# Moving the 64-row products of an MLP's first half next to the 64-row products of a recurrent cell

## The chip, the cores and the metric

The kernel runs on one core of a Trainium2 chip. Its engines work in parallel, each in its own order of instructions, and meet at semaphores: TensorE (PE in the profile) does matrix products, VectorE (DVE) and ScalarE (ACT) work element by element, GpSimd (POOL) does the same[...], and SyncE (SP) issues the transfers (DMAs). Products read their operands from SBUF and write to PSUM[...]. The metric is the device time of one execution in microseconds; the time of a kernel is the median of its runs.

## The reference

Two blocks follow each other, both in float32. The first is an mLSTM cell for 4 batches, 8 heads, 768 steps and a head size of 40. In essence:

```python
for t in range(S):
    m_new = np.maximum(f_gate[:, :, t] + m, i_gate[:, :, t])
    f_stab = np.exp(f_gate[:, :, t] + m - m_new)
    i_stab = np.exp(i_gate[:, :, t] - m_new)
    C = f_stab * C + i_stab * outer(v[t], k[t])
    n = f_stab * n + i_stab * k[t]
    y[t] = sigmoid(o[t]) * (C @ q[t]) / max(abs(n @ q[t]), 1)
```

The heads are then put side by side into x, 768 rows of 320 for each batch. The second block mixes and applies an MLP:

```python
u = x + real(fft(fft(x, axis=1), axis=2))
un = (u - mean(u)) / sqrt(var(u) + 1e-06)      # over the last axis
out = u + maximum(un @ w_ch1, 0) @ w_ch2       # 320 -> 1280 -> 320
```

## The kernel before, in words

**The recurrent cell** is computed in chunks: 768 steps are six chunks of 128 (c = 0 to 5). Within a chunk the steps act on each other through a 64-row matrix of scores, and the past comes in through a state. For batches 2 to 4 a chunk is treated as two halves of 64 steps, so that all its products are small ones of 64 or 40 rows on a quarter of PE's array (`product`, L519). A *recurrent group* is what PE does for one chunk in one slot: `halves_from_state` (L683), `halves_from_chunk` in two turns (L694), with a tiny read by ACT between them (`halves_between`, L699) and, with them, the next chunk's `halves_scores` (L635) and `halves_to_state` (L643). Around it, DVE adds to the state (`halves_add`, L667), weighs the scores (`halves_weigh`, L672) and makes the output (`mlstm_finish`, L712 to L720); POOL lets the state decay (`halves_decay`, L652), scales the queries (qg, L501) and the values (vw, L507) and masks (L515); ACT makes exponentials. The rows of the output that lie one step off are moved by SyncE and POOL in `halves_rows` (L731, L732).

**The mix** folds x into even and odd parts on DVE (`mix_fold`, L815 to L822; for later batches also `mix_fold_again`), transforms along both axes with products on PE, adds on DVE (`mix_add`, L952 to L966) and turns the centred result over, into the feature-major arrays `uT`.

**The MLP's first half** multiplies 320 features by 320x1280 weights. 320 is 128 + 64 + 128 rows: two *full* products of 128 rows and one *rest* of 64 rows. Two rests share PE's array, each in its own half of the rows (`w1t_sb` holds them). The 1280 hidden features form ten blocks of 128, taken in pairs n = 0 to 4; the 768 rows form two groups (gr = 0, 1) of 384. For batch 1, `mlp_in` (L1059) issues the full products of a pair, and its inner function `between` (L1050) the pair's rests behind them, or at the start of the next pair. For batches 2 to 4, `mlp_block` does a pair in four steps in the manner of Strassen: seven full products (L1121) in place of eight, with sums of the weights and of the inputs; the sums of inputs come from DVE (`mlp_sums`, L1109: T3 in buffer e, uT in place, T2 in buffer raw, T4 in buffer m). Step 2 ends with four rests (`tails`, L1126) and with three additions on DVE (`add`, L1130). Four PSUM banks, pm0 to pm3, hold the results; the first product of pair i + 1 (`begin`) takes the bank of pair i that `add(h12, p3)` has read last.

**Order.** Everything is in one order that is written by hand: `at(slot, phase, function, ...)` puts a call into a plan and `run` issues the calls sorted by slot and phase, the phases being EVAC 0, FILL 1, MAIN 2 and FILL_PE 3 with fractions between. Each engine executes its instructions in that order. A slot is roughly one step of an MLP. Batch 1's MLP begins at slot 31, the next ones 32 slots later each. The recurrent cell of batch b + 1 and its mix run in the slots of batch b's MLP: the cells begin at slots 32, 53 and 83, a chunk every three slots (`plan_halves`). `x_done` are the slots from which the mix may fold. The PSUM banks that the first MLP takes are written out as a string of digits (`turn`, in `bank`).

Of the kernel before, what the change touches and what calls it, by code (L numbers as in the profile page):

```python
# [19 lines left out]
L = 128  # L20
# [33 lines left out]
def kernel(  # L54
# [69 lines left out]
    def at(slot, phase, fn, *args):  # L124
        plan.setdefault((slot, phase), []).append((fn, args))
# [633 lines left out]
            at(t, FILL_PE + (2.5 if c < 4 else 1), mlstm_turn, b, c, c < 4)  # L759
            at(x, FILL + 0.05, mlstm_finish, b, c)  # L760

    def plan_halves(b, s0, stride=3):
        for c in range(NT):
            s = s0 + stride * c
            t = 22 + 2 * c if b == 1 and c < 3 else s - 5
            at(t, FILL, mlstm_load, b, c)
            at(t, FILL, mlstm_load_max, b, c)
            at(34 if b == 1 and c == 2 else t + 1, FILL, mlstm_load_decay, b, c)
            at(s - 1, FILL, mlstm_load_o, b, c)
            at(s - 1, FILL, mlstm_scale_v, b, c)  # L770
            at(s - 1, FILL + 0.3, mlstm_exp, b, c, 0)
            at(s, FILL, mlstm_exp, b, c, NP)
            at(s, FILL_PE + 2.05, halves_scores, b, c)
            at(s, FILL_PE + 2.5, halves_to_state, b, c)
            for i in range(2):
                at(s + i, FILL + 0.05, halves_decay, b, c, i)
                at(s + 1 + i, FILL - 0.2, halves_add, b, c, i)
            at(s, FILL + 0.1, mlstm_scale_q, b, c)
            at(s + 1, FILL, mlstm_mask, b, c)
            if (b, c) == (3, 2):  # L780
                at(s + 2, MAIN + 0.1, halves_weigh, b, c)
            else:
                at(s + 1, FILL + 0.55 if b == 1 and c > 0 else MAIN + 0.7, halves_weigh, b, c)
            end = c == NT - 1
            at(s + 3, MAIN - 0.1 if end else FILL_PE, halves_from_state, b, c)
            at(s + 3, MAIN - 0.1 if end else FILL_PE, halves_from_chunk, b, c, 0)
            at(s + 3, MAIN if end else FILL_PE + 0.5, halves_between, b, c)
            at(s + 3, FILL_PE + 3, halves_from_chunk, b, c, 1)
            at(s + 3, FILL_PE + 0.6, mlstm_tanh, b, c)
            at(s + (5 if (b, c) == (2, 2) else 4), {(2, 4): FILL + 0.3, (3, 3): FILL - 0.3}.get((b, c), FILL + 0.3 if b == 1 else MAIN + 0.55), mlstm_finish, b, c)  # L790
            at(s + 6, FILL - 0.6, halves_rows, b, c)

    class Mix:
        def __init__(self):
            self.pu, self.uc, self.pt, self.po = {}, {}, {}, {}

    mixes = {}  # L800

# [208 lines left out]
    def plan_mix(b, s0, x_done, s_feat, s_add, s_turn):  # L1010
        for j in range(TG):
            p = TG - 1 - j
            at(x_done[j] + (b > 1 and j == TG - 1), FILL + 0.5 if b < 2 else FILL_PE + 0.2, mix_fold, b, p)
            if b == 0:
                at((s0 - 4, s0 - 2, s0)[j], FILL_PE + 4, mix_seq, b, p, (0, 1))
                at((s0 - 2, s0 - 2, s0)[j], FILL_PE + 4, mix_tail, b, p)
            elif b == 1 or j == 0:
                if b > 1:
                    for step, slot in enumerate((x_done[0], x_done[-1] + 2, x_done[-1] + 6)):
                        at(slot, FILL_PE + 0.25, mix_fold_again, b, step)  # L1020
                at(s0, FILL_PE + 4, mix_seq, b, p, (0,))
                at(s0 + 1, FILL_PE + 4, mix_seq, b, p, (1,))
                at(s0 + 2, FILL_PE + 4, mix_tail, b, p)
        for i in range(2):
            at(s0 + 1 if b == 0 else s0 + 1 + i, FILL, mix_seq_out, b, i)
        at(s0 + (1 if b == 0 else 3), FILL + 0.1, mix_tail_out, b)
        for p in range(TG):
            at(s_feat[p], FILL_PE + 4, mix_feat, b, p)
        for c, a, t in zip(ORDER, s_add, s_turn):
            at(a, FILL if b < 2 else MAIN - 0.3 if c == 0 else MAIN + 0.5, mix_add, b, c)  # L1030
            at(t, FILL + 0.1, mix_center, b, c)
            at(t, FILL_PE + (5 if b == 0 or c in ORDER[:4] else -0.1), mix_turn, b, c)
            if b > 0:
                at(t, FILL_PE + 6, mix_turn_out, b, c)
            elif t < s_mlp:
                at(t + 1, FILL + 0.2, mix_turn_out, b, c)
            else:
                at(t + 1, EVAC, mix_turn_out, b, c)


    def mlp_in(b, gr, f):


        k = mixes[b]
        u = [uT_bufs[gr][:, ch].rearrange("p c t -> p (c t)") for ch in range(3)]

        def between(pm, n, start):
            for i in range(2):
                r = slice(i * TAIL, (i + 1) * TAIL)
                nc.tensor.matmul(pm[i], w1t_sb[r, n * L:(n + 1) * L], u[1][r], start=start, stop=not start,  # L1050
                                 skip_group_check=True)


        ahead = gr == 1 and f // 2 in (1, 3)
        if f % 2 == 0:
            k.pm = k.pm_next if ahead else [bank("pm", [L, TG * L]) for _ in range(2)]
        for i, ch in ((1, 1),) if f % 2 else ((0, 0), (0, 1), (1, 0)):
            f0 = (f // 2 * 2 + i) * L
            nc.tensor.matmul(k.pm[i], w1_sb[:, ch, f0:f0 + L], u[2 * ch], start=(ch == 0 and not ahead),  # L1059
                             stop=(ch == 1 and ahead), skip_group_check=True)  # L1060
        if f % 2 and not ahead:
            between(k.pm, f // 2, False)
            if gr == 1 and f // 2 < NFF // 2 - 1:
                k.pm_next = [bank("pm", [L, TG * L]) for _ in range(2)]
                between(k.pm_next, f // 2 + 1, True)


    hid = {}
# [1 line left out]
    def hidden(gr, f):  # L1070
        return hid[gr, f % 2][:, f // 2 * TG * L:(f // 2 + 1) * TG * L]

    def mlp_relu(b, gr, f):
        nc.scalar.activation(out=hidden(gr, f), in_=mixes[b].pm[f % 2], func=AF.Relu, scale=-1.0)

# [35 lines left out]
    def mlp_block(b, i, step):  # L1111
# [30 lines left out]
        if step == 0:  # L1142
            if i == 0:
                begin(0)
            k.pm = [k.p1, bank("pm", [L, TG * L], banks[1])]
            product(k.pm[1], A[0, 1], mlp_u(0, 2), True)
        elif step == 1:
            k.pm.append(bank("pm", [L, TG * L], banks[2]))
            p1, _, p5 = k.pm
            if i == 0:  # L1150
                product(p5, A[1, 0], mlp_u(1, 0), True)
            product(p1, block(w1x["S2"], i), T2)
            nc.scalar.copy(out=h12, in_=p1)
            if i > 0:
                product(p5, A[1, 0], mlp_u(1, 0), True)
            add(h12, p5)
        elif step == 2:
            k.pm.append(bank("pm", [L, TG * L], banks[3]))
            p1, p2, p5, p3 = k.pm
            product(p3, block(w1x["S4"], i), mlp_u(1, 2), True)  # L1160
            product(p1, block(w1x["S3"], i), T3)
            nc.scalar.copy(out=h22, in_=p1)
            tails(1, (p3, p5))
            tails(0, (p2, p1))
            add(h12, p3)
# [326 lines left out]
```

## Time and profile before

Three runs took 391.72 us in the median (391.14 to 392.08). The profiled execution took 392.19 us, 390.4 of them in the span that the profile covers.

| | before |
|---|---|
| median of the runs | 391.72 us |
| profiled execution | 392.19 us |
| span of the profile | 390.4 us |
| PE busy | 379.6 us, 4174 products |
| DVE busy | 278.0 us |
| ACT busy | 172.1 us |
| POOL busy | 134.9 us |
| granted clock of PE | full in all slices |

The first halves of the MLPs of batches 1, 2 and 3 lie, together with recurrent groups, at about 59 to 112, 163 to 204 and 249 to 286 us of the span. In these stretches PE is busy for 52.37 of 53.00, 40.36 of 41.00 and 36.16 of 37.00 us. Batch 4's MLP follows to the end, at 390.4 us.

In a line of the timeline, the first number is the start in microseconds from the beginning of the span, the second the length, then come engine, line of the kernel, operation and operands; `128*128` is the part of PE's array that a product uses (rows by columns), and `[0.35 <-DVE uT L1109]` an idle time ahead of the line and what ended it. A float32 product appears as two records. The ends of products are modelled, so starts are more exact than ends.

### The profile page before, as it was taken

The numbers are of one execution on the slowest core, as the hardware profiler recorded it, in microseconds if no ns is written. First come the engines' busy times: TensorE is split into PE (matmuls) and PEld (weight loads), VectorE is DVE, ScalarE is ACT, GpSimd is POOL, SyncE is SP. The second block draws the span as 40 slices with busy tenths as digits, with TensorE's granted clock in tenths as the row PEclk, the third lists the DMA queues.
The fourth block names the chain that finished last, engine by engine and source line by source line (L and its number), as shares of the span: only waits on it lengthen the run. The fifth ranks groups of instructions, "written<-read, shape, count | busy, mean of one in ns | idle before, by whom it ended". The sixth has DMA issues, their size and how long they took to land.

```text
span 390.4 us, 10585 instructions
## 1 busy us (share of the span) xinstructions
PE 379.6 (97%) x4174; PEld 277.3 (71%) x4174; DVE 278.0 (71%) x671; ACT 172.1 (44%) x481; POOL 134.9 (35%) x237
## 2 busy tenths in 40 slices
PE   8999899999999999999999999999999999999996
PEld 6777555656667777765569998755588996556996
DVE  7789988499599587476975699777655785346652
ACT  6887357477543233655462314554530133545000
POOL 5739504467954442173254134541500000020000
PEclk9999999999999999999999999999999999999999
DMA  7887499579394345437700626400000000000101
GB/s 224 287 235 204 159 254 255 179 214 271 109 231 116 122 116 150 149 102 184 182 2 28 174 80 192 135 20 2 0 2 34 6 30 34 2 0 0 35 34 35
DMA packets 25631, 44.78 MB, mean 115 GB/s; under 512 B 5727, under 2 KB 14766, under 8 KB 25454
## 3 DMA queue, kind: packets, MB, share of 16 engines
q1 hardware_dynamic: 25582, 44.11, 38.9%
q8 instruction: 33, 0.54, 0.6%
q14 instruction: 16, 0.13, 0.1%
HBM read 38.49 MB, written 4.12 MB: 109 GB/s over the span
## 4 chain that ended last, share of the span: by engine, by line
PE 78%; DVE 14%; issue 3%; ACT 3%; POOL 1%; DVEq 0%; ACTq 0%; POOLq 0%
PE po L1240 20%; PE pm L1121 15%; PE po L1184 8%; PE pm L1059 7%; PE ph L519 4%; PE pm L1126 4%; PE pu L938 4%; PE ps L519 3%; PE pm L1050 2%; PE put L981 2%; PE pz L907 1%; PE pz L895 1%; DVE h L1130 1%; DVE so L716 1%; PE pM L221 1%
## 5 line engine op out<-in xcount | busy, mean ns | idle before, releaser
L1190 DVE SCALAR_TENSOR_TENSOR x<-po,rstd,x 128x160 f32<-128x160 f32 (+1 forms) x69 | 27.1, 394 | 37.4 <-PE po L1240 32.5
L1130 DVE TENSOR_TENSOR h<-h,pm 128x384 f32<-128x384 f32 x60 | 30.5, 548 | 27.1 <-PE pm L1121 12.6
L652 POOL TENSOR_TENSOR C<-C,decB 128x164 f32<-128x164 f32 x30 | 15.9, 531 | 67.5 <-DVE C L667 56.1
L1121 PE MATMUL pm<-uT,w_sb 128*128 128x384 f32 x90 | 37.7, 506 | 1.3 <-DVE uT L1109 0.6
L491 ACT ACTIVATE W<-W,colT 128x64 f32<-128x64 f32 x144 | 37.5, 339 | 0.4 <-DMA W<-M_d 0.4
L1184 PE MATMUL po<-w_sb,h 128*128 128x320 f32 x120 | 34.3, 435 | 0.0
L515 POOL TENSOR_SCALAR_AFFINE_SELECT W<-W 64x512 f32<-64x512 f32 x36 | 27.3, 759 | 10.6 <-ACT W L491 9.1
L1005 POOL TENSOR_TENSOR t<-rstd 128x6 f32<-128x6 f32 x12 | 3.3, 273 | 79.9 <-DVE v L999 79.4
L1059 PE MATMUL pm<-uT,w_sb 128*128 128x384 f32 x80 | 29.2, 500 | 0.1
L1184 PEld LDWEIGHTS po<-w_sb,h 128*128 128x128 f32 x120 | 22.3, 190 | 9.5 <-issue 0.6
L1240 PE MATMUL po<-T,S 128*128 128x160 f32 x180 | 27.8, 301 | 0.3 <-DVE x L1190 0.3
L501 POOL TENSOR_TENSOR qg<-qk,Gb 128x512 f32<-128x512 f32 (+1 forms) x21 | 27.1, 1290 | 1.7 <-DMA qk<-in_qkT 1.6
L1240 PEld LDWEIGHTS po<-T,S 128*128 128x128 f32 x180 | 25.5, 190 | 1.7 <-DVE x L1190 0.5
L1121 PEld LDWEIGHTS pm<-uT,w_sb 128*128 128x128 f32 x90 | 15.5, 189 | 15.6 <-DVE h L1130 6.7
L1240 PE MATMUL po<-w_sb,h 128*128 128x160 f32 x180 | 26.3, 300 | 0.0
L1240 PEld LDWEIGHTS po<-w_sb,h 128*128 128x128 f32 x180 | 25.2, 190 | 1.4 <-DVE x L1190 0.3
L986 ACT COPY uT<-put 128x384 f32<-128x384 f32 x24 | 11.2, 477 | 30.1 <-PE put L981 30.1
L507 POOL TENSOR_TENSOR vw<-kvt,colT 128x328 f32<-128x328 f32 x23 | 19.7, 859 | 13.1 <-DMA qk<-in_qkT 10.1
L1177 ACT ACTIVATE h<-h 128x384 f32<-128x384 f32 x45 | 23.1, 520 | 2.0 <-DVE h L1130 2.0
L1126 PE MATMUL pm<-uT,w1t_sb 64*128 64x384 f32 x120 | 23.4, 508 | 0.0
L1059 PEld LDWEIGHTS pm<-uT,w_sb 128*128 128x128 f32 x80 | 14.1, 189 | 9.6 <-issue 1.9
L974 ACT ACTIVATE uc<-x 128x384 f32<-128x384 f32 x24 | 14.4, 613 | 12.6 <-DVE x L966 11.1
(241 smaller groups left out, 843.4 us busy)
## 6 DMA issues: line engine op xcount, KB each, us to landing
kvt<-in_kv SPq DMA_DIRECT2D x24, 336.0 KB
qk<-in_qkT SPq DMA_DIRECT2D x48, 160.0 KB
raw<-in_w SPq DMA_DIRECT2D x10, 640.0 KB
Gb<-G_d SPq DMA_DIRECT2D x36, 128.0 KB
W<-M_d SPq DMA_DIRECT2D x36, 128.0 KB
so<-in_o SPq DMA_DIRECT2D x24, 160.0 KB
out<-x SPq DMA_DIRECT2D x24, 160.0 KB
x<-so SPq DMA_DIRECT2D x9, 140.0 KB
```

The costliest lines, as they stand in the source:

```text
L491: nc.scalar.activation(out=k.W[:, h, :], in_=M, func=AF.Exp, scale=-1.0, bias=colT[:, c, 0, b * H + h:b * H + h + 1])
L501: nc.gpsimd.tensor_tensor(out=k.qg[:, :, t], in0=k.qk[:, 0, :, t], in1=k.Gb[:, :, t], op=OP.mult)
L515: nc.gpsimd.affine_select(out=W, in_=W, compare_op=OP.is_ge, fill=0.0, base=base, pattern=[[0, H], [step, LH]], channel_multiplier=-1)
L519: nc.tensor.matmul(out, w, x, start=start, stop=True, skip_group_check=True)
L1059: nc.tensor.matmul(k.pm[i], w1_sb[:, ch, f0:f0 + L], u[2 * ch], start=(ch == 0 and not ahead), stop=(ch == 1 and ahead), skip_group_check= ...
L1121: nc.tensor.matmul(bank, w, u, start=start, stop=True, skip_group_check=True)
L1126: nc.tensor.matmul(bank, block(w1t_sb, i)[rows], mlp_u(gr, 1)[rows], start=False, stop=True, skip_group_check=True)
L1130: nc.vector.tensor_tensor(out=h, in0=h, in1=bank, op=OP.add)
L1177: nc.scalar.activation(out=h, in_=h, func=AF.Relu, scale=-1.0)
L1184: nc.tensor.matmul(k.po[gr, i], hidden(gr, f)[:, i * L:(i + 1) * L], w2_sb[:, f, :], start=(f == 0), stop=(f == NFF - 1))
L1190: nc.vector.scalar_tensor_tensor(out=u, in0=po, scalar=k.rstd[:, c:c + 1], in1=u, op0=OP.mult, op1=OP.add)
L1240: nc.tensor.matmul(po, a[:, f], w[:, f], start=start and f == 0, stop=f == half - 1, skip_group_check=True)
```

## The change

Rests move to recurrent groups, or recurrent groups to rests. No product is added or removed, and each is computed on the same operands.

1. *Batch 1.* `between` goes. A new function `mlp_tails` issues the two rests of a pair, and a table of slots puts it ahead of or behind recurrent groups. `TAILS_AHEAD` lists the pairs whose rests open the sum in the bank, `TAILS_BEHIND` those whose rests close it; for the others they come in the middle. The banks are kept by pair (`k.pm`), and the last relus of the first group of rows stand one slot later.
2. *Batches 2 to 4, MLP.* In `mlp_block`, the rests and the three additions become a step of their own (3) in the same slot, at phase MAIN + 0.05; what was step 3 becomes step 4. Slots are counted as before.
3. *Cells of batches 3 and 4.* `plan_halves` takes the starts of the chunks from a table in place of a stride of three. Batch 3's last two groups come one and two slots later, batch 4's last three 2, 3 and 4 slots later. A chunk's output groups stand at the next chunk's start (`o`), and the last one at MAIN + 0.02, just ahead of the rests.
4. `x_done` of batch 4 and the last step of `mix_fold_again` are fitted to that.

```diff
-    def plan_halves(b, s0, stride=3):
+    def plan_halves(b, s0):
+        starts = [s0 + n for n in ((0, 3, 6, 9, 12, 15, 18), (0, 3, 6, 9, 12, 16, 20), (0, 3, 6, 9, 14, 18, 22))[b - 1]]
         for c in range(NT):
-            s = s0 + stride * c
+            s, o = starts[c:c + 2]
...
-            at(s + 3, MAIN - 0.1 if end else FILL_PE, halves_from_state, b, c)
-            at(s + 3, MAIN - 0.1 if end else FILL_PE, halves_from_chunk, b, c, 0)
-            at(s + 3, MAIN if end else FILL_PE + 0.5, halves_between, b, c)
-            at(s + 3, FILL_PE + 3, halves_from_chunk, b, c, 1)
-            at(s + 3, FILL_PE + 0.6, mlstm_tanh, b, c)
-            at(s + (5 if (b, c) == (2, 2) else 4), {(2, 4): FILL + 0.3, (3, 3): FILL - 0.3}.get((b, c), FILL + 0.3 if b == 1 else MAIN + 0.55), mlstm_finish, b, c)
-            at(s + 6, FILL - 0.6, halves_rows, b, c)
+            at(o, MAIN + 0.02 if end else FILL_PE, halves_from_state, b, c)
+            at(o, MAIN + 0.02 if end else FILL_PE, halves_from_chunk, b, c, 0)
+            at(o, MAIN + 0.03 if end else FILL_PE + 0.5, halves_between, b, c)
+            at(o, FILL_PE + 3, halves_from_chunk, b, c, 1)
+            at(o, FILL_PE + 0.6, mlstm_tanh, b, c)
+            at(o + (2 if (b, c) == (2, 2) else 1), {(2, 4): FILL + 0.3, (3, 3): FILL - 0.3}.get((b, c), FILL + 0.3 if b == 1 else MAIN + 0.55), mlstm_finish, b, c)
+            at(o + 3, FILL - 0.6, halves_rows, b, c)
...
-                    for step, slot in enumerate((x_done[0], x_done[-1] + 2, x_done[-1] + 6)):
+                    for step, slot in enumerate((x_done[0], x_done[-1] + 2, x_done[-1] + (6 if b == 2 else 5))):
...
-        def between(pm, n, start):
...
-        ahead = gr == 1 and f // 2 in (1, 3)
-        if f % 2 == 0:
-            k.pm = k.pm_next if ahead else [bank("pm", [L, TG * L]) for _ in range(2)]
+        if f % 2 == 0 and (gr, f // 2) not in k.pm:
+            k.pm[gr, f // 2] = [bank("pm", [L, TG * L]) for _ in range(2)]
+        pm, ahead, tailed = k.pm[gr, f // 2], (gr, f // 2) in TAILS_AHEAD, (gr, f // 2) in TAILS_BEHIND
...
-        if f % 2 and not ahead:
-            between(k.pm, f // 2, False)
-            if gr == 1 and f // 2 < NFF // 2 - 1:
-                k.pm_next = [bank("pm", [L, TG * L]) for _ in range(2)]
-                between(k.pm_next, f // 2 + 1, True)
...
+    TAILS_AHEAD, TAILS_BEHIND = ((0, 1), (1, 2)), ((0, 0), (0, 3), (0, 4), (1, 1), (1, 4))
+
+    def mlp_tails(b, gr, n):
+
+        k = mixes[b]
+        ahead, last = (gr, n) in TAILS_AHEAD, (gr, n) in TAILS_BEHIND
+        if ahead:
+            k.pm[gr, n] = [bank("pm", [L, TG * L]) for _ in range(2)]
+        for i in range(2):
+            r = slice(i * TAIL, (i + 1) * TAIL)
+            nc.tensor.matmul(k.pm[gr, n][i], w1t_sb[r, n * L:(n + 1) * L], uT_bufs[gr][r, 1].rearrange("p c t -> p (c t)"),
+                             start=ahead, stop=last, skip_group_check=True)
...
             nc.scalar.copy(out=h22, in_=p1)
+        elif step == 3:
+            p1, p2, p5, p3 = k.pm
             tails(1, (p3, p5))
             tails(0, (p2, p1))
             add(h12, p3)
...
-            for step in range(4):
-                at(s, MAIN, mlp_block, b, i, step)
-                s += 1
+            for step in range(5):
+                at(s, MAIN + 0.05 * (step == 3), mlp_block, b, i, step)
+                s += step != 2
...
-                    at(s, EVAC, mlp_relu, b, gr, f - 1)
-                    at(s, EVAC, mlp_relu, b, gr, f)
+                    late = gr == 0 and f == NFF - 1
+                    at(s + late, EVAC, mlp_relu, b, gr, f - 1)
+                    at(s + late, EVAC, mlp_relu, b, gr, f)
+        if b == 0:
+            for slot, phase, gr, n in ((1, 0.05, 0, 0), (1, 4.5, 0, 1), (4, 0.05, 0, 2), (7, 0.05, 0, 3), (10, 0.05, 0, 4),
+                                       (10, 0.05, 1, 0), (13, 0.05, 1, 1), (13, 0.05, 1, 2), (16, 0.05, 1, 3), (19, 0.05, 1, 4)):
+                at(s_mlp + slot, MAIN + phase, mlp_tails, b, gr, n)
...
-        done = [s_mlstm + n for n in ((16, 19, 22) if b == 0 else (18, 21, 22))]
+        done = [s_mlstm + n for n in ((16, 19, 22) if b == 0 else (20, 23, 24) if b == 3 else (18, 21, 22))]
```

More of the change, by code (lines that the diff above doesn't have):

```diff
@@ L784, in plan_halves @@
             end = c == NT - 1
-            at(s + 3, MAIN - 0.1 if end else FILL_PE, halves_from_state, b, c)
-            at(s + 3, MAIN - 0.1 if end else FILL_PE, halves_from_chunk, b, c, 0)
-            at(s + 3, MAIN if end else FILL_PE + 0.5, halves_between, b, c)
-            at(s + 3, FILL_PE + 3, halves_from_chunk, b, c, 1)
-            at(s + 3, FILL_PE + 0.6, mlstm_tanh, b, c)
-            at(s + (5 if (b, c) == (2, 2) else 4), {(2, 4): FILL + 0.3, (3, 3): FILL - 0.3}.get((b, c), FILL + 0.3 if b == 1 else MAIN + 0.55), mlstm_finish, b, c)
-            at(s + 6, FILL - 0.6, halves_rows, b, c)
+            at(o, MAIN + 0.02 if end else FILL_PE, halves_from_state, b, c)
[5 more added lines that the diff above has]
+            at(o + 3, FILL - 0.6, halves_rows, b, c)
     class Mix:
         def __init__(self):
-            self.pu, self.uc, self.pt, self.po = {}, {}, {}, {}
+            self.pu, self.uc, self.pt, self.po, self.pm = {}, {}, {}, {}, {}
     mixes = {}
@@ L1045, in mlp_in @@
         u = [uT_bufs[gr][:, ch].rearrange("p c t -> p (c t)") for ch in range(3)]
-        def between(pm, n, start):
[L1048 to L1051, printed above, removed]
-        ahead = gr == 1 and f // 2 in (1, 3)
-        if f % 2 == 0:
-            k.pm = k.pm_next if ahead else [bank("pm", [L, TG * L]) for _ in range(2)]
+        if f % 2 == 0 and (gr, f // 2) not in k.pm:
+            k.pm[gr, f // 2] = [bank("pm", [L, TG * L]) for _ in range(2)]
+        pm, ahead, tailed = k.pm[gr, f // 2], (gr, f // 2) in TAILS_AHEAD, (gr, f // 2) in TAILS_BEHIND
         for i, ch in ((1, 1),) if f % 2 else ((0, 0), (0, 1), (1, 0)):
             f0 = (f // 2 * 2 + i) * L
-            nc.tensor.matmul(k.pm[i], w1_sb[:, ch, f0:f0 + L], u[2 * ch], start=(ch == 0 and not ahead),
-                             stop=(ch == 1 and ahead), skip_group_check=True)
-        if f % 2 and not ahead:
-            between(k.pm, f // 2, False)
-            if gr == 1 and f // 2 < NFF // 2 - 1:
-                k.pm_next = [bank("pm", [L, TG * L]) for _ in range(2)]
-                between(k.pm_next, f // 2 + 1, True)
+            nc.tensor.matmul(pm[i], w1_sb[:, ch, f0:f0 + L], u[2 * ch], start=(ch == 0 and not ahead),
+                             stop=(ch == 1 and not tailed), skip_group_check=True)
+    TAILS_AHEAD, TAILS_BEHIND = ((0, 1), (1, 2)), ((0, 0), (0, 3), (0, 4), (1, 1), (1, 4))
[8 more added lines that the diff above has]
+                             start=ahead, stop=last, skip_group_check=True)
     hid = {}
@@ L1073, in mlp_relu @@
     def mlp_relu(b, gr, f):
-        nc.scalar.activation(out=hidden(gr, f), in_=mixes[b].pm[f % 2], func=AF.Relu, scale=-1.0)
+        nc.scalar.activation(out=hidden(gr, f), in_=mixes[b].pm[gr, f // 2][f % 2], func=AF.Relu, scale=-1.0)
     def block(t, n):
```

## The prediction

> **What bounds the kernel now.** First the page's head, its busy shares and its chain by engine, to see whether one engine sets the end.
>
> ```profile
> span 390.4 us, 10585 instructions
> PE 379.6 (97%) x4174; PEld 277.3 (71%) x4174; DVE 278.0 (71%) x671; ACT 172.1 (44%) x481; POOL 134.9 (35%) x237
> PE 78%; DVE 14%; issue 3%; ACT 3%; POOL 1%; DVEq 0%; ACTq 0%; POOLq 0%
> ```
>
> TensorE (PE) is busy for 97% of the span and carries most of the chain. So a nanosecond saved in PE's stream shortens the run, if nothing PE waits for becomes late. "Busy" includes the gaps in which PE changes the shape of its products, so they must be read from starts of instructions. The timeline of PE in batch 1's MLP, taken line by line (start, length, engine, group):
>
> ```profile
> 75.50 0.92 PE L1050 MATMUL pm<-uT,w1t_sb 64*128 64x384 f32 x4
> 76.35 0.55 PE L981 MATMUL put<-ident,uc 128*128 128x128 f32 x3
> 76.73 2.75 PE L1059 MATMUL pm<-uT,w_sb 128*128 128x384 f32 x8
> 79.41 0.92 PE L1050 MATMUL pm<-uT,w1t_sb 64*128 64x384 f32 x4
> 80.25 0.68 PE L519 MATMUL ph<-C,qg 40*64 40x41 f32 x32
> ```
>
> Rests (64*128, called T below) stand between full products (F, 128*128), recurrent groups (R, 64*64 and 40*64) elsewhere. One fp32 product is two records. From one record's start to the next: full to full 322.5 ns, but last full to first rest 416 (+93); first pair of rests to the next 420 instead of 316 (+104): entering T costs 197 ns. Leaving T costs 97 + 104 = 201. T to R costs 97 + 22 = 119, F to R 93 + 22 = 115, R to F 118 + 104 = 222. R to T occurs nowhere: bounds 115 (the cheapest switch seen) and 319 (R's exit and both parts of T's entry, 118 + 201); I take 222, as R to F.
>
> Next the waits that come near PE: VectorE (DVE) in the first-half stages. PE, then DVE, then POOL at the start of batch 3's MLP:
>
> ```profile
> 248.40 1.45 PE L1121 MATMUL pm<-uT,w_sb 128*128 128x384 f32 x4
> 249.78 0.68 PE L519 MATMUL ph<-C,qg 40*64 40x41 f32 x32
> 250.27 0.42 PE L519 MATMUL ph<-kvt,W 64*64 64x41 f32 x16
> 250.50 0.67 PE L519 MATMUL ps<-qk 40*64 40x64 f32 x32
> 251.00 0.51 PE L519 MATMUL ps<-vw,kvt 64*40 64x41 f32 x32
> 251.32 0.42 PE L519 MATMUL ph<-kvt,W 64*64 64x41 f32 x16
> 252.08 0.91 PE L1121 MATMUL pm<-uT,w_sb 128*128 128x384 f32 x2 [0.35 <-DVE uT L1109]
> ```
>
> ```profile
> 249.65 0.81 DVE L1109 TENSOR_TENSOR e<-uT 128x384 f32<-128x384 f32 x1
> 250.50 1.53 DVE L1109 TENSOR_TENSOR uT<-uT,uT 128x384 f32<-128x384 f32 x1
> 252.06 0.88 DVE L1109 TENSOR_TENSOR raw<-uT 128x384 f32<-128x384 f32 x1
> ```
>
> ```profile
> 249.59 0.46 POOL L652 TENSOR_TENSOR C<-C,decB 128x164 f32<-128x164 f32 x1
> 250.02 1.59 POOL L501 TENSOR_TENSOR qg<-qk,Gb 128x512 f32<-128x512 f32 x1
> 251.57 1.90 POOL L515 TENSOR_SCALAR_AFFINE_SELECT W<-W 64x512 f32<-64x512 f32 x2
> ```
>
> A recurrent group fills the time in which DVE forms the sums that PE needs. Those sums take 0.81, 1.53 and 0.88 us; alone (batch 2, from 163.87) each takes 0.56. Their ends follow POOL's: the two engines alternate.
>
> **What the Trainium skill says.** "TensorEngine Tiling (Array Packing)", Key Properties: changing the tiling mode drains TensorE, changing the tile within a mode does not. The trace agrees: 93 to 118 ns at every change of shape, and 7 ns between the two row halves of a pair of rests. "TensorE: Matmul & The Clock Gate", Part 3, The mechanism: weights are loaded ahead only where the row groups do not conflict; here the load of 79.408 starts 2 ns before its product, after a switch. "SBUF — State Buffer", Who interferes with whom: a DVE instruction with two SBUF inputs contends with a GpSimd one that reads SBUF, and the first to start holds the port for its whole length; the 1.53 us beside qg's 1.59 agree.
>
> **The change part by part.** No product is added or removed; the rests are moved until they touch recurrent groups. Counting neighbours in the order of PE's instructions, before and after: F to T 23 to 19, R to F 23 to 19, F to R 19 to 11, T to F 18 to 10, T to R 5 to 13, R to T 0 to 4. The sum is −4×0.197 − 4×0.222 − 8×0.115 − 8×0.201 + 8×0.119 + 4×0.222 = −2.36 us: 12 switches fewer, 0.197 each, six in batch 1's MLP, three each in batch 2's and 3's. With R to T at 115 ns it is −2.79, at 319 it is −1.97.
>
> Batch 1's MLP (59 to 112 us): −1.18. The first product of group (0,3) used to follow a pair of rests; now it directly follows the recurrent group. Its bank is read by DVE's L958 of the mix, which ends at 76.06 where R ended at 74.50. Before, PE came to it 2.23 us after R; now 2.23 minus the rests and their switches (about 0.94) = 1.29, while DVE frees the bank at 1.56 plus a handover of 0.07: a wait of +0.34. Behind it on PE stands the rest of the stage. Other covers thin without vanishing: the weighing (L672) of chunk 4 ends at 103.68 for a use at 104.83 and PE comes 0.98 earlier; the last piece of the second weights (L426) ends 0.6 to 0.75 ahead of need. ACT's warm-up wait of 0.50 at 82.48 stays. Net −0.84 (bounds −1.18 if the bank is free in time, −0.4 if the last cover goes too).
>
> Batch 2's MLP (163 to 204): −0.59 of switches. Gone with the order: two lags of 0.063 into the next block (179.69, 187.56) and a warm-up wait of about 0.4 (176.75): −0.52. New: batch 3's last finish (L712 to L720) stands, in block 3, ahead of the folding. DVE's queue from the last rest of block 2 to the release of block 3's first bank:
>
> ```profile
> 192.75 1.56 PE L1126 MATMUL pm<-uT,w1t_sb 64*128 64x384 f32 x8
> 194.53 0.91 PE L1121 MATMUL pm<-uT,w_sb 128*128 128x384 f32 x2 [0.21 <-DVE h L1130]
> ```
>
> DVE needs 1.27 (adds) + 1.59 (finish) + 1.59 (fold) + 0.90 (L1212) + 0.55 (L994 to L999) + 0.46 (add) + 1.59 (fold) + 0.60 (add and handover) = 8.56 us; PE is there after R8 0.78 + fourteen full records 4.30 + rests 1.50 + switches 0.41 = 6.99. PE waits 1.57 instead of 0.29: +1.28. Net +0.17.
>
> Batch 3's MLP (249 to 286): the group at 249.78 now stands two slots later. PE is free at 249.69 and the sums stand bare. POOL's order becomes the two one-row copies (L731, L732), vw of chunk 4 (L507), decay, qg. The copies end at 249.6, DVE's L1190 at 249.74: I take vw as first. It holds the port for about 0.65 of its median 0.74 us (records overlap by some 0.1), to 250.25; then in turn e 0.5 (to 250.75), decay 0.35, uT 0.5 (to 251.6), qg 1.0 (my estimate of its part not spent waiting, from the median of 1.27), raw 0.55 (to 253.15); the product with raw starts at 253.2: stalls of 2.87 us against 0.59 before, +2.28. Without the group's DVE and POOL work three waits fall (257.20, 262.69, 273.28: 0.38 + 0.16 + 0.15 = −0.69). Block 3 has the same late finish without L1212: 7.65 − 6.99 = 0.66 against 0.06, +0.60. Switches −0.59. Net +1.60. If DVE starts first, raw is ready at 252.1 and the net is +0.5.
>
> Batch 4's MLP is unchanged. DMA issues move with the groups, on SyncE: the loads of batch 3's last chunk and of batch 4's chunks 4 and 5 by one to three slots, as far as their readers do; the row moves of batch 4's chunk 3 by two slots, three slots ahead of the fold that reads them. DMA engines are busy for 8% of 249 to 286 us and hide them. Without that cover a landing would delay that fold; the page gives no landing time, so the bounds are nothing and one slot, about 1.5 us. I take nothing.
>
> Sum: −0.84 + 0.17 + 1.60 = +0.93 us on the profiled 392.19 (span 390.4 and 1.8 outside it). The median shown, 391.72, lies 0.47 below, so the forecast is 391.72 + 0.93, about 392.6.
>
> **The rivals.** Measurement can tell 0.2%, 0.78 us, from no change.
> 1. The switches are saved and the waits are covered: PE's lead in these stages is made by DVE work that moves away together with the group, so the sums stand earlier than I placed them, and the finish slips behind the add. For it: DVE is only 71% busy, and half of my +2.28 hangs on POOL. Against: PE reaches the sums at 249.69 and DVE starts them at 249.65. It decides if the product with raw starts before about 251.4. Then stage sums −1.0, −0.9, 0: about 389.9, faster: the other side.
> 2. DVE comes before vw in the tie at 249.6 (60 ns apart): stage three +0.5 and a total of −0.2: 391.5.
> 3. DVE's backlog does not drain, and the copies on ACT (L1153, L1162) start behind exps and hold the banks longer: another 0.5 to 1 us in blocks 2 and 3: 393.5.
> 4. A saved switch is worth less, because R to T drains at 319 ns and not 222: +0.39, about 393.0; a shade of the likeliest case.
>
> **How the numbers follow.** The likeliest case with rival 4, 392.6 ± 0.5: 0.42. Rival 1, 389.9 ± 0.7: 0.28. Rival 2, 391.5 ± 0.4: 0.22. Rival 3: 0.08. From 389.6 to 393.5 no more than two tenths are left out; the likeliest case's own range is 392.0 to 393.2. Slower (over 392.5): 0.24 + 0.02 + 0.08 = 0.34. Same: 0.18 + 0.16 + 0.01 = 0.35. Faster: 0.27 + 0.04 = 0.31.
>
> **What would show it.** Switches: R to T near 222 ns, twelve fewer in all. Stage one: a wait of 0.2 to 0.5 us on L958 at about 75.5, and the stage 0.8 shorter. Stage two: DVE L1130 releases PE at block 3 after a wait of over 1 us. Stage three: PE idle for 2 to 3 us on L1109, sums alternating with vw, decay and qg. I am wrong if those waits are below 1 us in sum, or if a wait turns up in batch 4's MLP, whose order does not change.

## The result

The changed kernel takes 394.79 us in the median of 5 runs (393.66 to 395.70), beside 391.75 us for the kernel before (391.14 to 392.08): a ratio of 1.0076, with a 95% interval of 1.0063 to 1.0088. It is 3.0 us slower. The forecast was 392.6 us with a range up to 393.5, so it had the change too cheap by 2.2 us.

The page of the changed kernel, with the lines that answer to the first ones shown of before:

```profile
span 393.1 us, 10579 instructions
PE 378.7 (96%) x4174; PEld 278.2 (71%) x4174; DVE 278.7 (71%) x671; ACT 172.0 (44%) x481; POOL 134.9 (34%) x237
PE 77%; DVE 12%; issue 3%; POOL 3%; ACT 2%; DMA 1%; SPq 0%; DVEq 0%; POOLq 0%; ACTq 0%
```

TensorE is busy for 0.9 us less than before (378.7 against 379.6), yet the span is 2.7 us longer. So time has gone from TensorE's work into TensorE's waits, and more of it than was saved. To place it, I compare the start of the same product in both traces and take the difference as an offset. The first product of the recurrent group at 63.16 us is a start common to both, and the others lie behind each first half. What a stage costs is the growth of the offset over it:

| product (start before) | offset after | the stage's share |
|---|---|---|
| first group, 63.16 | −0.01 | |
| in batch 1's second half, 126.09 | +0.57 | batch 1: +0.58 (forecast −0.84) |
| behind batch 2's first half, 205.07 | +0.92 | batch 2: +0.35 (forecast +0.17) |
| behind batch 3's first half, 287.04 | +2.69 | batch 3: +1.77 (forecast +1.60) |

The three add up to the 2.7 us by which the span grew; batch 4's MLP adds nothing. Two of the three stages came out near the forecast. The error is in batch 1's.

Shares and medians do not agree to better than some tenths of a microsecond, for a reason that lies ahead of the first group. Up to there all kernels of this document issue the same work, and yet their profiled executions differ. Eight equal products near the start, in the traces of before (the changed kernel's trace has the same line) and of the last run below:

```profile
4.75 1.91 PE L221 MATMUL pM<-w_sb,ident 128*128 128x128 f32 x8
```

```profile
4.74 1.27 PE L221 MATMUL pM<-w_sb,ident 128*128 128x128 f32 x8
```

They begin 213 ns apart at first, and 111 ns apart once the trace's record of the granted clock sets in, which is at 7.08 us in the one and at 5.17 us in the other. (The view by slices, "full in all slices", does not show this.) In the last run it moves all that follows 0.71 us to the front, where the runs of before spread over 0.94 us. Medians contain this, shares do not; so a difference of half a microsecond is read from shares here.

TensorE's timeline in batch 1's MLP, after:

```profile
72.58 0.92 PE L1066 MATMUL pm<-uT,w1t_sb 64*128 64x384 f32 x4
...
76.85 2.82 PE L1053 MATMUL pm<-uT,w_sb 128*128 128x384 f32 x8 [0.31 <-DVE x L959]
...
83.12 0.44 PE L519 MATMUL ph<-kvt,W 64*64 64x41 f32 x16 [0.95 <-ACT warm L699]
...
110.25 0.92 PE L1066 MATMUL pm<-uT,w1t_sb 64*128 64x384 f32 x4
111.80 0.44 PE L519 MATMUL ph<-kvt,W 64*64 64x41 f32 x16 [0.64 <-ACT warm L699]
```

The wait on L959 (L958 before) was forecast. The one at 83.12 was 0.50 us and is 0.95 now, and the one at 111.80 was not there. The same two products before:

```profile
82.48 0.44 PE L519 MATMUL ph<-kvt,W 64*64 64x41 f32 x16 [0.50 <-ACT warm L699]
...
111.36 0.44 PE L519 MATMUL ph<-kvt,W 64*64 64x41 f32 x16
```

By starts, up to the next change of shape, the three cost 0.55, 0.45 and 0.71 us more than without them or than before; two small waits at 90.5 and 97.6 us are gone (0.18 us in sum), and the groups at 104.2 and 109.4 us take 0.06 us longer. That makes 1.59 us against the 1.18 saved on changes of shape. Where do the two ACT waits come from? VectorE at the end of the recurrent group behind 72.58, first before, then after:

```profile
74.63 0.33 DVE L667 TENSOR_TENSOR C<-C,ps 128x164 f32<-128x164 f32 x1 [2.64 <-PE ps L519]
```

```profile
75.27 0.33 DVE L667 TENSOR_TENSOR C<-C,ps 128x164 f32<-128x164 f32 x1 [3.48 <-PE ps L519]
```

It starts 0.64 us later, since a pair of rests now stands ahead of the group and not behind it. From here on VectorE is never idle for more than 0.3 us until 98 us, in either trace, and ACT's read (L699) at 83 us lies behind an activation that waits for VectorE. After:

```profile
80.11 0.83 ACT L413 ACTIVATE e<-e,ebias 128x640 uint32<-128x640 uint32 x1 [1.34 <-DVE e L406]
...
82.93 0.13 ACT L699 COPY warm<-ph 1x1 f32<-1x1 f32 x1
```

From this L667 to the product that waits at 82.48 or 83.12 it is 7.85 us in both. The chain goes on. At 96.9 us VectorE hands it to POOL, which then works without a gap of 0.1 us until it has masked (L515) at 109.1; from there it runs through VectorE and ACT to the last wait. POOL, VectorE and ACT after:

```profile
96.88 0.78 POOL L1006 TENSOR_TENSOR t<-rstd 128x6 f32<-128x6 f32 x1 [2.14 <-DVE v L1000]
```

```profile
109.13 0.69 DVE L672 TENSOR_TENSOR W<-ps,W 128x512 f32<-128x512 f32 x1 [0.74 <-POOL W L515]
```

```profile
110.26 0.83 ACT L413 ACTIVATE e<-e,ebias 128x640 uint32<-128x640 uint32 x1 [2.87 <-DVE e L406]
...
111.62 0.13 ACT L699 COPY warm<-ph 1x1 f32<-1x1 f32 x1
```

In the kernel before, these six stand at 79.47, 82.29, 96.25, 108.39, 109.52 and 110.88: the 0.64 us are passed on from link to link, and the mask adds 0.1. ACT's last read so comes 0.74 us later. The product behind it had 0.30 us of room before: it started 0.48 us after the read, where 0.18 is enough (111.62 to 111.80). So it must come 0.44 us later, and that is what the stage has lost by 112 us, 0.45. TensorE itself would have been there 0.26 us earlier than before; this lead, too, has gone into the wait.

Batch 3's MLP, TensorE, VectorE and POOL after, the same views as shown of before:

```profile
249.33 1.45 PE L1123 MATMUL pm<-uT,w_sb 128*128 128x384 f32 x4
252.45 0.91 PE L1123 MATMUL pm<-uT,w_sb 128*128 128x384 f32 x2 [1.67 <-DVE uT L1111]
254.09 0.88 PE L1123 MATMUL pm<-raw 128*128 128x384 f32 x2 [0.72 <-DVE raw L1111]
```

```profile
250.58 1.08 DVE L1111 TENSOR_TENSOR e<-uT 128x384 f32<-128x384 f32 x1
251.69 0.70 DVE L1111 TENSOR_TENSOR uT<-uT,uT 128x384 f32<-128x384 f32 x1
252.43 1.51 DVE L1111 TENSOR_TENSOR raw<-uT 128x384 f32<-128x384 f32 x1
```

```profile
250.52 0.72 POOL L507 TENSOR_TENSOR vw<-kvt,colT 128x328 f32<-128x328 f32 x1
251.21 0.77 POOL L652 TENSOR_TENSOR C<-C,decB 128x164 f32<-128x164 f32 x1
251.94 1.58 POOL L501 TENSOR_TENSOR qg<-qk,Gb 128x512 f32<-128x512 f32 x1
```

The recurrent group is gone from between the products, vw comes first (by 0.06 us), and each sum ends behind a POOL instruction. By starts, TensorE loses 2.72 us here, against 0.59 before.

Batch 2's MLP, TensorE in block 3 after:

```profile
192.34 2.60 PE L1128 MATMUL pm<-uT,w1t_sb 64*128 64x384 f32 x8
195.45 0.91 PE L1123 MATMUL pm<-uT,w_sb 128*128 128x384 f32 x2 [0.50 <-DVE h L1132]
```

Only 0.50 us is marked as idle, but the eight records of rests take 2.60 us where they took 1.56 before; a second wait lies inside them, for the addition that reads a bank they write to. VectorE's additions after:

```profile
192.79 0.55 DVE L1132 TENSOR_TENSOR h<-h,pm 128x384 f32<-128x384 f32 x1
...
194.85 1.47 DVE L1132 TENSOR_TENSOR h<-h,pm 128x384 f32<-128x384 f32 x3
```

The third of the eight records starts at 193.39, 0.05 us behind the end of the first line, and block 4's first product starts the same 0.05 us behind the first of the three additions. Together it is 1.61 us by starts.

### The profile page after: what moved, and what is told of

Same layout as the page of the kernel before. It is cut to its first block, busy times and chain, and to the rows that moved or that the text cites. A ratio compares the mean times of both kernels' runs of the same rounds, so it can differ in the third digit from the quotient of the medians.

```text
span 393.1 us, 10579 instructions
## 1 busy us (share of the span) xinstructions
PE 378.7 (96%) x4174; PEld 278.2 (71%) x4174; DVE 278.7 (71%) x671; ACT 172.0 (44%) x481; POOL 134.9 (34%) x237
## 4 chain that ended last, share of the span: by engine, by line
PE 77%; DVE 12%; issue 3%; POOL 3%; ACT 2%; DMA 1%; SPq 0%; DVEq 0%; POOLq 0%; ACTq 0%
PE po L1244 19%; PE pm L1123 16%; PE po L1188 8%; PE pm L1128 5%; PE ph L519 4%; PE pu L939 4%; PE pm L1053 3%; PE ps L519 3%; PE put L982 2%; PE pz L908 1%; PE pz L896 1%; PE pM L221 1%; DMA Gb<-G_d 1%; PE pm L1066 1%; PE pi L139 1%
## 5 line engine op out<-in xcount | busy, mean ns | idle before, releaser
L1123 PE MATMUL pm<-uT,w_sb 128*128 128x384 f32 x90 | 37.5, 504 | 3.0 <-DVE uT L1111 1.9
L515 POOL TENSOR_SCALAR_AFFINE_SELECT W<-W 64x512 f32<-64x512 f32 x36 | 27.2, 756 | 15.5 <-ACT W L491 11.1
L1053 PE MATMUL pm<-uT,w_sb 128*128 128x384 f32 x80 | 28.2, 496 | 0.4 <-DVE x L959 0.3
L1128 PE MATMUL pm<-uT,w1t_sb 64*128 64x384 f32 x120 | 24.9, 511 | 0.1
```

What stands on the lines that cost most here:

```text
L515: nc.gpsimd.affine_select(out=W, in_=W, compare_op=OP.is_ge, fill=0.0, base=base, pattern=[[0, H], [step, LH]], channel_multiplier=-1)
L1053: nc.tensor.matmul(pm[i], w1_sb[:, ch, f0:f0 + L], u[2 * ch], start=(ch == 0 and not ahead), stop=(ch == 1 and not tailed), skip_group_che ...
L1123: nc.tensor.matmul(bank, w, u, start=start, stop=True, skip_group_check=True)
L1128: nc.tensor.matmul(bank, block(w1t_sb, i)[rows], mlp_u(gr, 1)[rows], start=False, stop=True, skip_group_check=True)
```

## The experiments

Two theories stood against each other for batch 1. *A:* the recurrent group at 72 us starts a chain through VectorE, POOL and ACT that is as long as TensorE's own work; a later start of the group delays all that follows, and what TensorE saves in between turns into waiting. *B:* TensorE's stream sets the stage, as predicted, and the lost time lies elsewhere. A third, *C:* every pair of rests ahead of a group costs for itself. "Share" below is again the growth of the offset over a stage, from the trace; ratios are to the kernel before, run beside it.

**Batch 1's part alone.** The starts, `x_done` and the end phases of batches 3 and 4 are as before (the first lines of the edit):

```diff
-        starts = [s0 + n for n in ((0, 3, 6, 9, 12, 15, 18), (0, 3, 6, 9, 12, 16, 20), (0, 3, 6, 9, 14, 18, 22))[b - 1]]
+        starts = [s0 + n for n in (0, 3, 6, 9, 12, 15, 18)]
...
```

> Batch 1's part of the change alone; the cells and MLPs of batches 2 to 4 as before. Theory A (VectorE's unbroken work from the recurrent group at 72 us to the last ACT read at 111 us sets the length of batch 1's stage, and that group now starts 0.64 us later, behind a pair of rests): 0.5 to 0.6 us slower than before, about 392.3. Theory B (TensorE's stream sets it, as predicted): 0.84 us faster, about 390.9.

Measured 392.61 us beside 392.09, ratio 1.0008 (1.0000 to 1.0016); batch 1's share is +0.44 us, the other stages are as before. No gain appears, where B expected 0.84 us. Of the 0.58 in the changed kernel's trace, 0.13 arose in the second half, at 124 to 126 us; two of the runs below show it too (batch 4's chunk 3 back, and the last folds moved), this one and the others do not.

**The rests (0,2) behind the group.** On top of that:

```diff
-            for slot, phase, gr, n in ((1, 0.05, 0, 0), (1, 4.5, 0, 1), (4, 0.05, 0, 2), ...
+            for slot, phase, gr, n in ((1, 0.05, 0, 0), (1, 4.5, 0, 1), (4, 4.5, 0, 2), ...
```

> As the run of batch 1's part alone, but with the one pair of rests (0,2) behind its recurrent group and not ahead of it; the number of changes of shape is the same. Theory A (the group's end starts VectorE's chain): the chain starts 0.2 us earlier than before, all later waits shrink with it, about 0.8 us under batch 1's part alone: 391.2 to 391.6. Rival C (every pair of rests ahead of a group delays its own group and costs for itself): only one of six is taken away, 0.1 to 0.2 us under batch 1's part alone, about 392.1.

Measured 391.46 us beside 392.09, ratio 0.9991 (0.9982 to 0.9999); batch 1's share is −0.40 us, 0.84 less than above, from moving two products past one group. VectorE's start and the wait behind it:

```profile
74.08 0.32 DVE L667 TENSOR_TENSOR C<-C,ps 128x164 f32<-128x164 f32 x1 [2.64 <-PE ps L519]
```

```profile
81.92 0.44 PE L519 MATMUL ph<-kvt,W 64*64 64x41 f32 x16 [0.65 <-ACT warm L699]
```

It is 7.84 us from one to the other again, and the product behind the last wait stands 36.54 us behind L667, as in the changed kernel (36.54) and in the run above (36.53):

```profile
110.61 0.44 PE L519 MATMUL ph<-kvt,W 64*64 64x41 f32 x16 [0.64 <-ACT warm L699]
```

So the last wait has not shrunk: the whole stage has moved with the group. By places, 0.55 of the 0.84 us is the wait on L959, which is gone, and 0.30 the wait at 81.92. A freed bank alone would not have helped, though, because TensorE still waits for ACT behind it. C is out, since the other rests still stand ahead of their groups.

**The group earlier, and nothing else.** The kernel before, with the group of chunk 0's outputs ahead of slot 35's three full products and not behind them; the phases of its seven calls change in this way:

```diff
-            at(s + 3, MAIN - 0.1 if end else FILL_PE, halves_from_state, b, c)
...
+            first = (b, c) == (1, 0)
+            at(s + 3, FILL + 0.8 if first else MAIN - 0.1 if end else FILL_PE, halves_from_state, b, c)
...
```

> The kernel before, with one edit: the recurrent group that stood behind the three full products of slot 35 (at 72.8 us) stands ahead of them, 1.9 us earlier. No change of shape is saved, no rest is moved. Theory A (this group starts VectorE's chain, which sets the waits at 82.5, 90.5 and 97.6 us): these waits, 0.7 us in sum, go, and the time is 0.5 to 0.8 us under before. Theory B (TensorE's own work sets the stage, the waits are local): no difference to before, within 0.2 us.

Measured 390.93 us beside 391.72, ratio 0.9978 (0.9971 to 0.9985); batch 1's share is −0.86 us. One change of shape is saved here after all: the group now follows four products on a single column of the array (128*1, at 70.0 us), which had a change behind them anyway. That is 0.20 us. The waits are nearly gone:

```profile
72.42 0.33 DVE L667 TENSOR_TENSOR C<-C,ps 128x164 f32<-128x164 f32 x1 [0.51 <-PE ps L519]
```

```profile
81.74 0.44 PE L519 MATMUL ph<-kvt,W 64*64 64x41 f32 x16
```

VectorE starts 2.2 us earlier, and the product that waited 0.50 us for ACT has no idle time marked ahead of it. By starts, this wait is 0.47 us shorter (the group takes 2.13 us in place of 2.60, and 1.88 where nothing is waited for), and the two small ones at 90.5 and 97.6 us are gone (0.19). With the change of shape this is the whole 0.86. B allows the 0.20, not the 0.66 of waits that go without any work being removed. The chain set the stage already before the change; B falls.

**Batch 1's part, with that group ahead and the rests (0,2) opening their banks behind it.**

```diff
-    TAILS_AHEAD, TAILS_BEHIND = ((0, 1), (1, 2)), ((0, 0), (0, 3), (0, 4), (1, 1), (1, 4))
+    TAILS_AHEAD, TAILS_BEHIND = ((0, 1), (0, 2), (1, 2)), ((0, 0), (0, 3), (0, 4), (1, 1), (1, 4))
...
-    (4, 0.05, 0, 2)
+    (4, -0.1, 0, 2)
```

> Batch 1's part of the change, with the same group ahead of slot 35's full products and the rests (0,2) behind the group, opening their banks; batches 2 to 4 as before. Theory A: with the chain out of the way, six saved changes of shape (1.18 us) and the old waits (0.7 us) both count: 1.4 to 2.0 us under before. Theory B: at most the 1.18 us.

Measured 390.51 us beside 391.72, ratio 0.9969 (0.9960 to 0.9979); batch 1's share is −1.55 us. That is the 0.86 of the earlier group and the 1.18 of saved changes of shape, less a wait of 0.44 for ACT (0.37 by its mark) that stays ahead of the last 16 small products:

```profile
109.22 0.44 PE L519 MATMUL ph<-kvt,W 64*64 64x41 f32 x16 [0.37 <-ACT warm L699]
```

Now the saved changes count. The medians differ by 1.21 us only, less than the 1.4 expected, and with their interval (0.8 to 1.6 us) could not tell A from B; the trace can.

**Batch 4's chunk 3 back at slot 95**, in the changed kernel:

```diff
-(0, 3, 6, 9, 14, 18, 22)
+(0, 3, 6, 9, 12, 18, 22)
```

> The changed kernel, with the group of chunk 3 of batch 4 back at slot 95, at the start of batch 3's MLP. Theory A (that group covered TensorE's wait for VectorE's sums): the idle time of 2.7 us at 250 to 254 us falls to about 0.6, one more change of shape costs 0.2, and the wait of 0.4 for an addition behind the first rests may come back: 1.3 to 1.9 us under the changed kernel, 392.9 to 393.5. Rival (the idle time only moves to the next block, where the group's VectorE work is now missing or added): within 0.5 us of the changed kernel.

Measured 393.02 us beside 392.09, ratio 1.0024 (1.0016 to 1.0032); batch 3's share falls from +1.77 to +0.15 us. Both waits of before return to their old sizes:

```profile
253.05 0.91 PE L1123 MATMUL pm<-uT,w_sb 128*128 128x384 f32 x2 [0.35 <-DVE uT L1111]
...
258.16 0.91 PE L1123 MATMUL pm<-uT,w_sb 128*128 128x384 f32 x2 [0.31 <-DVE h L1132]
```

**POOL cleared of vw and qg**, in the changed kernel, by loading and scaling batch 4's chunk 4 three slots earlier:

```diff
+            early = 3 * ((b, c) == (3, 4))
-            t = 22 + 2 * c if b == 1 and c < 3 else s - 5
+            t = 22 + 2 * c if b == 1 and c < 3 else s - 5 - early
...
-            at(s - 1, FILL, mlstm_scale_v, b, c)
+            at(s - 1 - early, FILL, mlstm_scale_v, b, c)
...
-            at(s, FILL + 0.1, mlstm_scale_q, b, c)
+            at(s - early, FILL + 0.1, mlstm_scale_q, b, c)
```

> The changed kernel, with batch 4's chunk 4 loaded, its values scaled and its queries scaled three slots earlier, so that POOL has only two one-row copies and one state decay left beside VectorE's sums at the start of batch 3's MLP. Theory A (POOL's reads and the sums with two SBUF inputs take turns): the sums shrink from 1.08, 0.70 and 1.51 us to 0.6 to 0.9 each, the idle time of 2.7 us to 1.1 to 1.5: 1.2 to 1.6 us under the changed kernel. Rival (the sums are late because VectorE comes to them late): the idle time stays above 2.3 us, within 0.4 us of the changed kernel.

Measured 393.04 us beside 391.72, ratio 1.0033 (1.0021 to 1.0045); batch 3's share falls from +1.77 to +0.42 us. VectorE's sums:

```profile
250.44 0.81 DVE L1112 TENSOR_TENSOR e<-uT 128x384 f32<-128x384 f32 x1
251.29 0.56 DVE L1112 TENSOR_TENSOR uT<-uT,uT 128x384 f32<-128x384 f32 x1
251.88 0.56 DVE L1112 TENSOR_TENSOR raw<-uT 128x384 f32<-128x384 f32 x1
```

One POOL instruction is left beside them (the decay, from 250.38), and only the first sum is longer than 0.56 us. TensorE:

```profile
251.90 0.91 PE L1124 MATMUL pm<-uT,w_sb 128*128 128x384 f32 x2 [1.26 <-DVE uT L1112]
```

By starts it loses 1.42 us here. So about half of the bare wait is POOL's. The other half is the time of the first two sums themselves: VectorE comes to them when TensorE is already there (in the changed kernel at 250.58, with TensorE done with its work at about 250.6).

**The last folds of batches 3 and 4 behind the additions of block 3**, in the changed kernel:

```diff
-            at(x_done[j] + (b > 1 and j == TG - 1), FILL + 0.5 if b < 2 else FILL_PE + 0.2, mix_fold, b, p)
+            at(x_done[j] + 2 * (b > 1 and j == TG - 1), FILL + 0.5 if b < 2 else FILL_PE + 0.2, mix_fold, b, p)
```

> The changed kernel, with the last fold of batches 3 and 4 behind the three additions of block 3 and not ahead of them; TensorE's order is the same. Theory A (the fold of 1.6 us in VectorE's queue holds the bank that block 4 begins with): the waits of 0.57 us at 195.4 and at 282.2 go, those inside the rests stay: about 1.1 us under the changed kernel, 393.5 to 393.9. Rival (VectorE's queue is late anyway, and the work behind the fold is late next): no difference, 394.8.

Measured 394.07 us beside 392.09, ratio 1.0052 (1.0039 to 1.0065). Batch 2's share falls from +0.35 to −0.23, the expected 0.57 us. Batch 3's rises from +1.77 to +2.06: the wait at 282.2 goes, and another stands at the first product of the outputs, which waits for the last additions.

```profile
288.16 1.08 PE L1244 MATMUL po<-w_sb,h 128*128 128x160 f32 x6 [0.58 <-DVE h L1132]
```

Theory A held in one stage, the rival in the other.

**Combinations.** The first joins batch 1 as in the run with −1.55, the change's cell of batch 3, and batch 4's cell as before, with one of the sums of output weights out of the way:

```diff
-        at((56, 57, 58, 75)[n], FILL + 0.4, out_weight_sums, n)
+        at((56, 57, 58, 79)[n], (FILL + 0.4, FILL + 0.4, FILL + 0.4, MAIN + 0.7)[n], out_weight_sums, n)
```

> The run before last's batch 1 (group earlier, rests behind it), the change's cell of batch 3 with the fourth sum of the output weights (L1216) moved from slot 75 to 79, and batch 4's cell as before the change. Theory A: 1.18 + 0.7 us in batch 1's MLP, 0.59 of changes of shape and 0.5 of waits in batch 2's, if block 3's additions no longer stand behind 1 us of other work: 2.2 to 3.0 us under before. Rival (the moved sum is late for the additions of block 4 or the outputs): 1.4 to 2.0 us under before.

Measured 389.57 us beside 391.72, ratio 0.9938 (0.9925 to 0.9952), 2.15 us and so at the lower edge of what A expected; shares −1.51, −0.55 and −0.20 us. The fold still holds back block 4:

```profile
192.47 0.91 PE L1124 MATMUL pm<-uT,w_sb 128*128 128x384 f32 x2 [0.50 <-DVE h L1133]
```

Then batch 3's last fold behind the additions (`x_done[j] + (2 if b == 2 else b > 1) * (j == TG - 1)`):

> The last combination with batch 3's last fold behind the three additions of block 3. Theory A (the wait of 0.57 us at 192.5 us is that fold in front of the additions): it goes, 0.5 us under that combination, 2.6 to 3.1 us under before. Rival (what stands behind the fold is late next, as it was in batch 3's MLP when the fold was moved there): no gain.

Measured 390.24 us beside 391.96, ratio 0.9956 (0.9945 to 0.9968); batch 2's share is −0.17 us, worse than −0.55: the rival's case. The wait moved into the rests of block 4, because fold and weight sum now both stand ahead of an addition that these rests wait for:

```profile
196.61 2.51 PE L1129 MATMUL pm<-uT,w1t_sb 64*128 64x384 f32 x8
```

And with that, batch 2's last group ahead of batch 1's last full product again, as before the change (`MAIN + 0.02 if b == 2 else MAIN - 0.1`):

> As that, and the last group of batch 2's cell stands ahead of the last full product of batch 1's first half again, as before the change: one change of shape more (0.2 us), but the product (0.65 us) lies in the wait for ACT of 0.47 us at 109.9. Theory A: the wait goes, 0.2 to 0.3 us less than without this edit, 2.8 to 3.4 us under before. Rival (ACT's read comes later with it): no difference or 0.2 us more.

Measured 389.64 us beside 391.96, ratio 0.9950 (0.9938 to 0.9962); batch 1's share is −1.44 against −1.54 us. The wait for ACT goes, one change of shape comes back, and a wait of 0.35 us for the weighing (L672) appears at 107.9: no gain by the shares. The median is 0.6 us lower than that of the run above, but the intervals of the ratios overlap widely. Last, the weight sum moved on to slot 82 in place of 79, without the edit before:

> As the combination with batch 3's last fold behind the additions of block 3, with the fourth sum of the output weights (L1216) moved on from slot 79 to 82, behind the last additions. Theory A (fold and sum together stood before block 4's addition, which the rests of block 4 wait for at 197.6 us): that wait of 0.5 us and the one at 192.5 us are both gone, batch 2's stage is 1.0 to 1.2 us shorter than before the change, the kernel 2.8 to 3.3 us under before. Rival (VectorE has no room left in this stage, so the sum is late for the outputs): a new wait at 200 to 205 us, no better than 2.4 us under before.

Measured 389.07 us beside 392.19, ratio 0.9922 (0.9909 to 0.9936): 3.1 us faster than before, and the fastest of all. Shares are −1.54, −1.13 and +0.05 us, 2.6 us in sum; the other 0.5 us is not the edits', as far as the trace shows, since this is the execution that starts 0.71 us ahead. Block 3's rests and what follows:

```profile
189.52 1.70 PE L1129 MATMUL pm<-uT,w1t_sb 64*128 64x384 f32 x8
191.15 0.91 PE L1124 MATMUL pm<-uT,w_sb 128*128 128x384 f32 x2
...
195.87 1.56 PE L1129 MATMUL pm<-uT,w1t_sb 64*128 64x384 f32 x8
```

Both waits are gone.

## Why the prediction was wrong

**Changes of shape: right.** The order of products gave twelve fewer, and the trace shows their prices. R to T, which had to be bounded between 115 and 319 ns, costs what I took: the first rest starts 157 ns after the last small product instead of 38 (+119), and the first pair takes 420 instead of 316 (+104), 223 in sum. One reading needs a correction. The load of weights at 79.408 us stands only 2 ns ahead of its product, but that does not show that loads run ahead only where the row groups do not conflict: between two full products, which both use all rows, the load at 77.060 us stands 321 ns ahead of its product at 77.381.

**Batch 1's MLP: wrong; this step failed.** It said −1.18 + 0.34 = −0.84, and measured +0.58. The wait on L959 is there, 0.31 us by its idle mark and 0.55 by starts. What failed is "Other covers thin without vanishing" and "ACT's warm-up wait of 0.50 at 82.48 stays". I measured the room of each cover against VectorE's times of before and moved only TensorE. But the same edit moved the recurrent group at 72.8 us to 73.4, and VectorE's work starts with that group's end. So the covers moved to the right by 0.64 to 0.74 us while TensorE moved to the left. The wait at 82.48 grew by 0.45 us and one of 0.71 us appeared at 111.80, 1.16 us that no term of the sum held. The cover of the second, ACT's read at 110.88, is not among those that the step looked at. Its room was 0.30 us, so even with the group where it was the stage could have become shorter by about 0.30 us only, not by 0.84 (an estimate from the starts of both traces). And the one wait that the sum did charge, on L959, sets nothing: TensorE waits for ACT behind it in any case. That the waits follow the group is shown by the runs with the rests behind it (−0.84 us, with the same 36.5 us from L667 to the last wait) and with the group alone earlier (−0.86 us against the kernel before, 0.66 of it waits). By starts 0.41 us of the stage are accounted for, by the chain 0.44, by offsets 0.45 at its end; the 0.13 at 124 to 126 is not explained.

**"So a nanosecond saved in PE's stream shortens the run": wrong for this stage.** The condition that I added, "if nothing PE waits for becomes late", was the whole of it. TensorE was busy for 52.37 of 53.00 us, and still the engines beside it set the pace: the waits at 82.5, 90.5 and 97.6 us (0.9 us in sum by starts, against 1.88 us for a group that does not wait) were the mark of a loop with no room, and I had read the first as a local wait.

**Batch 2's MLP: right in the main.** Forecast +0.17, measured +0.35. The late finish costs 1.61 us in block 3, where the sum said 1.57, though 1.04 of it lies inside the rests. What the sum lacked is 0.24 us in the rests of block 1, which wait for ACT's copy (L1164); I had named ACT's copies only in rival 3. The warm-up wait at 176.75 that goes was taken as 0.4 us and is 0.48 by starts.

**Batch 3's MLP: right in mechanism and size.** vw came before the first sum, by 0.06 us; that this tie fell so was a guess that came true, and rival 2 was the other side of it. Idle time on the sums grew by 2.13 us (forecast 2.28); block 3 lost 0.71 where it was to lose 0.66. The sum as a whole gave +1.60 for +1.77. The rests of this MLP's second block hold another 0.24 us for ACT's copy, which the sum lacked as well.

**The rivals.** 1 (waits covered, 389.9) and 2 (VectorE first) did not happen. 3 gave the nearest time, 393.5, for a reason that explains only some 0.5 us. None held a chain started by a moved group, although the prediction's own step counted that group's wait.

## What to carry to other kernels

An engine at 97% does not own a stage in which it waits, even briefly, for the same partner at each round: follow such a wait back to what starts the partner's work, and count how much an edit moves that start. When work is moved ahead of an instruction that feeds other engines, all that they do moves too, so covers have to be measured against shifted times on both sides. In this kernel, work that feeds nobody, put behind the instruction that feeds the others, made the saved nanoseconds count again. And a wait ahead of a later wait for the same chain costs nothing by itself: to remove it gains nothing until the chain moves.

## What the runs showed of the hardware

- A wait can hide inside a busy group: eight rests that take 1.56 us unhindered took 2.60 us (2.51 in another run) without an idle mark of their own, since some of their products waited for a bank (one started 0.05 us behind the addition that read it).
- VectorE's sums of two SBUF operands, 0.56 us alone, took 1.08, 0.70 and 1.51 us beside POOL's vw, decay and qg, and 0.81, 0.56 and 0.56 beside the decay alone. VectorE lost 1.36 us to this in one place, and TensorE with it 1.30 us (idle time of 2.72 against 1.42).
- The change of shape from small 64-row products to rests costs 223 ns, as much as the one from them to full products (222).
- Equal products at the start of the program begin 213 ns apart and later 111 ns apart. The change from one to the other came at 5.0 to 7.2 us of the span in the thirteen traces, and moved everything behind it by up to 0.71 us.
